# Relu² attention and mixture of depths on one core: chosen rows read back from DRAM instead of picked by matmul, in a new written-out order

## The chip, the cores and the metric

The kernel runs on one core of a Trainium2 chip. The metric is the time of one execution on the device in microseconds (us); lower is better. Five engines each run their own instructions in order: PE (TensorE, the matmuls), DVE (VectorE), ACT (ScalarE), POOL (GpSimd; here mostly the issue of DMAs) and SP (the issue of a few DMAs). They wait for one another by semaphores. PE writes its results into PSUM; DVE and ACT carry them from there to SBUF ("evict" them).

## The reference

Attention with squared relu over 8 batches, 12 heads, 448 tokens, 64 columns a head; its output, with the heads side by side as 768 columns, is x. Then, in each batch, the 128 tokens with the largest gate score go through a two-layer expert, and its result, weighted by a sigmoid, is added to their rows.

```python
scores = scale * q @ k.T                        # per head, scale = 1/sqrt(64)
x_heads = (np.maximum(scores, 0.0) ** 2 / S) @ v
x = heads side by side                          # [8, 448, 768]
s = x @ w_gate                                  # [8, 448]
for b in range(8):
    top_idx = the 128 tokens with the largest s[b]
    xe = x[b, top_idx]
    ye = np.maximum(xe @ w1, 0.0) @ w2          # 768 -> 1024 -> 768
    g = sigmoid(s[b, top_idx])
    out[b] = x[b];  out[b, top_idx] += g[:, None] * ye
```

## The kernel before

**Units.** The work is cut into 24 units: four heads of one batch each, unit u being the heads 4(u mod 3) to 4(u mod 3)+3 of batch u // 3. The 448 tokens of a unit are seven chunks of 64. One PSUM tile `ps` has eight banks, which the order hands out by number.

**The order** is written out by hand: ORDER is a list of tokens, and each token is a call that puts its instructions on one engine. Nothing reorders them; each engine has the tokens that concern it, in the order of the list. In the names below u is a unit, b a batch, c a chunk, and a last letter A or D says that ACT or DVE evicts. Evictions go through `put`, so in a profile of the kernel before their line is that of the helper: L209 for ACT, L211, L213 and L215 for DVE.

- `L,q,u`, `L,k,u`, `L,v,u` (L107) and `W` (L130): loads on POOL, cast to bf16 on the way. POOL's DMAs go round eight semaphores, and an issue waits for the DMA before it on the same one. q and k of unit 0 come by SP as float32 (`LFq`, L115; `LFk`, L118) and are cast by DVE (`Cq`, L195) and by DVE and ACT (`Ck`).
- `PW,n` (L202): n warm-up products of zeros on PE.
- `T,u,0` and `T,u,1` (L225): 14 transposes each, of q and of k, and `TE` their copy to `qkt`.
- `S,u,c` (L243): the scores of chunk c, four products of 448 columns; `R,u,c`: their relu eviction to `r_sb` (168 in all, ACT does them); `Q,u,c0,c1` (L257): the squares of chunks c0 to c1-1 on DVE, into `a_sb`, three instructions a unit; `V,u,c` (L264): four products with v, that sum over the chunks; `X,u` (L272): the eviction of the unit's output, columns down the partitions, to `xT_sb`.
- `RT,u` (L281): eight transposes of `xT_sb` to rows, `RE,u` (L289) their eviction to `x_rows`; `ST,b` (L305, L306): two DMAs that store the batch's rows in `out`.
- The gate and the choice: `g,b,i` (L326) six products with the gate weights, which stand repeated in `wg_rep`, so that each partition of PSUM gets the score row; `bc` its eviction to `bc_sb` (float32); `col` (L336) and `colE` (L341) the scores as columns, `rk` (L348), `cs0`, `cs` (L354, L360), `rank` (L365) the rank of every token, `hot` (L370) the one-hot matrix of the chosen tokens, `sel` (L376) and `sE` (L381) their indices `idx`.
- The expert: `xe,b,c` (L389): 24 products of `x_rows` with `hot`, which pick the chosen tokens' rows and transpose them; `xeE` their eviction to `xeT`; `gs` and `sig` (L404, L409) the weight; `h,b,f` (L416) six products with w1 each, `hE` their eviction; `y,b,f` (L432) products with w2, `yE` their eviction with the weight, to `gye`; `ADD,b` (L445): one indirect DMA on POOL that adds `gye` to the chosen rows of `out`.

The experts of a batch run among the attention of later units. Behind the last batch's `y` products only the last `yE` and `ADD,7` are left.

## Time and profile before

| | before |
|---|---|
| time, median of 3 runs (lowest to highest) | 206.81 us (206.43 to 207.01) |
| the profiled execution's own time | 206.75 us |
| span in its trace | 205.0 us |
| mean granted TensorE clock over the span | 0.989 |
| HBM read and written, over the span | 39.33 and 14.16 MB, 261 GB/s |

The trace covers the span; what lies between it and the profiled execution's own time, 1.75 us, is outside the trace. "Busy" is time in which an engine runs an instruction; PE's weight loads (PEld) run beside its products. A row "a 0.90 PE ps L225 x28" in the chain says that at a us the chain ran through 28 products of line 225 on PE for 0.90 us. A timeline's row can stand for several neighbouring instructions of one kind (x20), and its bracket says how long the engine was idle before it and what released it.

### The profile page before, as it was taken

How to read it: one execution, taken by the hardware profiler on the slowest of the kernel's cores; microseconds unless marked ns; L12 is line 12 of the kernel's file. 1: busy time of each engine (PE TensorE's matmuls, PEld its weight loads, DVE VectorE, ACT ScalarE, POOL GpSimd, SP SyncE). 2: the span in 40 equal slices, each digit the busy share in tenths (PEclk: the TensorE clock that was granted, in tenths of full speed). 3: DMA queues.
4: the chain of work that ended last, by engine and by line, in shares of the span. 5: the costliest groups of instructions: out<-in, count | busy, mean ns of one | idle time of the engine just before them, and what ended most of it. 6: DMA issues, size and time to landing. Idle time of an engine off the chain costs nothing.

```text
span 205.0 us, 7282 instructions
## 1 busy us (share of the span) xinstructions
PE 190.1 (93%) x3205; PEld 131.0 (64%) x3205; DVE 172.9 (84%) x285; ACT 170.8 (83%) x215; POOL 82.2 (40%) x120
## 2 busy tenths in 40 slices
...
GB/s 179 155 199 193 204 206 205 210 202 207 204 178 48 136 201 161 4 89 322 343 204 159 95 104 308 302 337 210 193 13 233 39 52 41 68 261 266 170 23 53
...
## 3 DMA queue, kind: packets, MB, share of 16 engines
...
q14 instruction: 6, 0.05, 0.1%
HBM read 39.33 MB, written 14.16 MB: 261 GB/s over the span
## 4 chain that ended last, share of the span: by engine, by line
PE 82%; DVE 8%; ACT 4%; issue 1%; POOLq 1%; DVEq 0%
PE ps L243 17%; PE ps L264 13%; PE ps L416 11%; PE ps L432 11%; PE ps L225 9%; PE ps L389 6%; PE ps L281 5%; DVE a_sb L257 4%; ACT r_sb L209 4%; PE ps L326 4%; PE ps L202 3%; DVE qkt L213 2%; PE ps L336 1%; POOLq L590 1%; DVE mask_sb L348 1%
## 5 line engine op out<-in xcount | busy, mean ns | idle before, releaser
L209 ACT ACTIVATE r_sb<-ps 128x896 bf16<-128x896 f32 x168 | 141.8, 942 | 8.7 <-PE ps L243 7.5
L257 DVE TENSOR_TENSOR a_sb<-r_sb 128x1792 bf16<-128x1792 bf16 (+1 forms) x72 | 87.1, 1238 | 0.0
L243 PE MATMUL ps<-qkt 64*64 64x448 bf16 x672 | 54.0, 360 | 2.6 <-ACT r_sb L209 0.9
L264 PE MATMUL ps<-a_sb,v_sb 64*64 64x448 bf16 x672 | 42.4, 351 | 0.4 <-ACT r_sb L209 0.2
L243 PEld LDWEIGHTS <-qkt 64*64 64x64 bf16 x672 | 20.8, 104 | 20.7 <-issue 10.3
L213 DVE COPY qkt<-ps 128x1792 bf16<-128x1792 bf16 (+1 forms) x24 | 25.5, 1068 | 2.7 <-PE ps L225 2.3
L264 PEld LDWEIGHTS <-v_sb 64*64 64x64 bf16 x672 | 20.7, 106 | 9.8 <-issue 1.5
L107 POOL DMA_DIRECT2D v_sb<-in_v_dram x24 | 17.4, 724 | 23.3 <-PE ps L243 18.6
L445 POOL DMA_INDIRECT out_dram<-gye,idx x8 | 13.4, 1675 | 32.6 <-DVE cols L341 8.8
L416 PE MATMUL ps<-xeT,w_sb 128*128 128x128 bf16 x384 | 25.0, 219 | 0.4 <-ACT xeT L209 0.4
L416 PEld LDWEIGHTS <-w_sb 128*128 128x128 bf16 x384 | 21.9, 98 | 4.9 <-issue 3.8
L107 POOL DMA_DIRECT2D q_sb<-in_q_dram x23 | 17.5, 761 | 18.2 <-PE ps L225 14.3
L432 PE MATMUL ps<-w_sb,hT 128*128 128x384 bf16 x128 | 24.7, 326 | 0.0
L107 POOL DMA_DIRECT2D k_sb<-in_k_dram x23 | 16.7, 729 | 9.7 <-PE ps L225 5.9
L215 DVE TENSOR_SCALAR xT_sb<-ps 128x896 bf16<-128x896 f32 x13 | 14.1, 1088 | 1.9 <-PE ps L264 1.6
L432 PEld LDWEIGHTS <-hT 128*128 128x128 bf16 x128 | 10.6, 97 | 7.3 <-issue 2.1
L225 PE MATMUL ps<-ident,q_sb 128*64 128x128 bf16 x336 | 14.1, 224 | 0.8 <-ACT r_sb L209 0.7
L225 PEld LDWEIGHTS <-q_sb 128*64 128x64 bf16 x336 | 10.7, 111 | 6.4 <-issue 4.9
L305 POOL DMA_DIRECT2D out_dram<-x_rows x8 | 5.0, 625 | 24.0 <-ACT r_sb L209 17.5
L281 PE MATMUL ps<-ident,xT_sb 128*128 128x128 bf16 x192 | 14.3, 220 | 0.0
L281 PEld LDWEIGHTS <-xT_sb 128*128 128x128 bf16 x192 | 11.2, 98 | 4.1 <-issue 3.0
L225 PE MATMUL ps<-ident,k_sb 128*64 128x128 bf16 x336 | 13.6, 219 | 0.0
...
## 6 DMA issues: line engine op xcount, KB each, us to landing
...
```

What stands on the lines that cost most here:

```text
L107: nc.gpsimd.dma_start(out=dst, in_=src(t, u))
L209: nc.scalar.activation(out=out_, in_=in_, func=func or AF.Copy, scale=scale)
L213: nc.vector.tensor_copy(out=out_, in_=in_)
L215: nc.vector.tensor_scalar(out=out_, in0=in_, scalar1=scale, scalar2=None, op0=ALU.mult)
L225: nc.tensor.matmul(out=PSB[HALF[j], bank, n * 128:(n + 1) * 128], lhsT=s[:, j, c, :], rhs=ident, is_transpose=True, start=(n == 0), stop=( ...
L243: nc.tensor.matmul(out=PS[HALF[hf], bank + j, :S], lhsT=qkt[u][HALF[j], 1, c, hf, :], rhs=qkt[u][HALF[j], 0, :, hf, :], start=True, stop=True)
L257: nc.vector.tensor_tensor(out=a_sb[u][:, c0:c1], in0=r, in1=r, op=ALU.mult)
L264: nc.tensor.matmul(out=PS[HALF[j], at["V", u] + hf, :S], lhsT=v_sb[u % NBUF][HALF[hf], j, c, :], rhs=a_sb[u][HALF[hf], c, j, :], start=(c ...
L281: nc.tensor.matmul(out=rows[:, c, g], lhsT=xT_sb[b % NX][:, 2 * uu + g, c, :], rhs=ident, is_transpose=True, start=(g == 0 and c == 0), st ...
L416: nc.tensor.matmul(out=PS[:, self.at["h"] + bk, o:o + 128], lhsT=w1_sb[:, m, f * 128:(f + 1) * 128], rhs=self.xeT[:, m, :], start=(m == 0) ...
L432: nc.tensor.matmul(out=PS[:, self.at["y"] + w, :384], lhsT=self.hT[:, f, :], rhs=w2_sb[:, f, w * 384:(w + 1) * 384], start=(f == 0), stop= ...
L445: nc.gpsimd.indirect_dma_start(out=out[0:self.b + 1].rearrange("b s d -> (b s) d"), out_offset=bass.IndirectOffsetOnAxis(ap=self.idx[:, :1 ...
```

## The change

1. **Chosen rows are read back.** For the batches 0 to 6 (READ), `XG,b` is an indirect DMA on POOL that reads the 128 chosen rows from `out`, where `ST,b` has stored them, into `xg` (bf16), and `XT,b` transposes `xg` by six products into PSUM. They take the place of the 24 products of `xe`. The read waits for `ST,b` and for `idx`; the transposes wait for the read. For batch 7 `xe` stays.
2. **Batch 7's scores** (DIRECT) come as columns straight from `xT_sb` (`colx`, 24 products of one column), and `rk` reads the score row in PSUM, so `bc` falls away there.
3. **The gate weights** are no longer repeated in SBUF: `g` reads one column of `wg_col` with stride 0 as its 128 columns. `wg_rep` and its two copies on DVE are gone.
4. **Opening.** SP loads k of unit 0 in two parts, chunks 0 to 1 and 2 to 6. q is cast by halves on DVE and ACT, and k's casts, transposes (`TK`) and copies (`TKE`) follow the two parts; q's copy is in two pieces, on ACT and DVE (`TQE`). There are 71 warm-up products in place of 75, 32 of them at the start in place of 40. The memsets of `xT_sb`, `bc_sb` and `mask_sb` go from DVE to POOL.
5. **Squares** in two instructions a unit, chunks 0 to 2 and 3 to 6.
6. **Last scatter** `ADD,7` as two DMAs, one for each half of the 768 columns; `between` puts a memset of one number (`gap`) on POOL ahead of an indirect DMA that follows another. Scatters and reads are declared independent of those of other batches.
7. **A new ORDER** for everything.

```diff
+    READ = (0, 1, 2, 3, 4, 5, 6)
+    DIRECT = (7,)
...
-    wg_rep = [const.tile([128, NM, 128], BF16, name=f"wg_rep{i}") for i in range(2)]
-    wg_col = const.tile([128, NM], BF16)
+    wg_col = const.tile([128, 2, NM], BF16)
...
-    def LFk():
-        nc.sync.dma_start(out=kf.rearrange("p j c d -> p j (c d)"), in_=src(k, 0))
+    def LFk(c0, c1):
+        nc.sync.dma_start(out=kf.rearrange("p j c d -> p j (c d)")[:, :, c0 * Dh:c1 * Dh],
+                          in_=src(k, 0)[:, :, c0 * Dh:c1 * Dh])
...
+    def between():
+
+        if last[0] in ("XG", "ADD"):
+            nc.gpsimd.memset(gap, 0.0)
...
-            nc.tensor.matmul(out=PS[:, self.at["g"], :S], lhsT=wg_rep[self.b not in BYDMA][:, i, :],
-                             rhs=self.xT[:, i].rearrange("p c n -> p (c n)")[:, :S], start=(i == 0), stop=(i == NM - 1),
-                             skip_group_check=True)
+            nc.tensor.matmul(out=PS[:, self.at["g"], :S],
+                             lhsT=wg_col[:, 1, i:i + 1].to_broadcast([128, 128]), rhs=self.xT[:, i].rearrange("p c n -> p (c n)")[:, :S],
+                             start=(i == 0), stop=(i == NM - 1), skip_group_check=True)
...
+        def colx(self, u, bank=None):
+            if u == 0:
+                self.at["col"] = bank
+            for m in (2 * u, 2 * u + 1):
+                for c in range(NR):
+                    nc.tensor.matmul(out=PS[:, self.at["col"], c:c + 1], lhsT=self.xT[:, m, c, :],
+                                     rhs=wg_col[:, 1 - (self.b in BYDMA), m:m + 1],
+                                     start=(m == 0 and c == 0),
+                                     stop=(m == NM - 1), skip_group_check=True)
...
+        def XG(self):
+            between()
+            self.xg = moe_pool.tile([CAP, HD], BF16, name="xg")
+            read = reads[self.b] = nc.gpsimd.indirect_dma_start(
+                out=self.xg, out_offset=None,
+                in_=out[0:self.b + 1].rearrange("b s d -> (b s) d"),
+                in_offset=bass.IndirectOffsetOnAxis(ap=self.idx[:, :1], axis=0),
+                element_offset=self.b * S * HD)
+            for b, add in adds:
+                tc.declare_no_dep(read.ins, add.ins, reason="rows of another batch")
+
+        def XT(self, bank):
+            self.at["xe"] = bank
+            for m in range(NM):
+                nc.tensor.matmul(out=PSB[:, bank, 128 * m:128 * m + 128],
+                                 lhsT=self.xg[:, 128 * m:128 * m + 128], rhs=ident,
+                                 is_transpose=True, start=(m == 0), stop=(m == NM - 1),
+                                 skip_group_check=True)
...
-        def ADD(self):
-            nc.gpsimd.indirect_dma_start(
-                out=out[0:self.b + 1].rearrange("b s d -> (b s) d"),
+        def ADD(self, part=None):
+            between()
+
+
+            w = 1 if part is None else 2
+            n = HD // w
+            add = nc.gpsimd.indirect_dma_start(
+                out=out[0:self.b + 1].rearrange("b s (w d) -> (b s w) d", w=w),
                 out_offset=bass.IndirectOffsetOnAxis(ap=self.idx[:, :1], axis=0),
-                in_=self.gye, in_offset=None, element_offset=self.b * S * HD,
-                compute_op=ALU.add)
+                in_=self.gye[:, (part or 0) * n:(part or 0) * n + n], in_offset=None,
+                element_offset=self.b * S * HD + (part or 0) * n, compute_op=ALU.add)
...
-    Zz PW,40,0 Zi Zs LFq LFk Ck,1 Cq T,0,0,0 Zt Ck,0 Zx PW,7,2 T,0,1 TE,0,1,D TE,0,0,A PW,13,2 S,0,0,0 R,0,0,A
+    LFq Zz LFk,0,2 Cq,0 Zi Zs Zt Ck,0,2,D PW,32,0 LFk,2,7 Cq,1 T,0,0,0 TQE,0,4,A TQE,4,7,D Zm TK,0,2 L,k,1 L,q,1
```

The new order shows best as each engine's own instructions. DVE at the very start, before (the names are the tiles written, and what they are read from):

```order
L136 MEMSET zero 128x64
L137 MEMSET unit_f 1x1
L195 CAST q_sb_83<-qf 128x896
L213 CAST k_sb_89<-kf 128x448
L146 MEMSET xT_sb_101 128x6x32
...
L148 MEMSET bc_sb_104 128x64
...
L213 COPY qkt<-ps 128x896
L176 CAST ident_119<-ident 6x6
L187 CAST wg_col<-ps 128x6
L188 CAST wg_rep_110<-ps 128x768
```

And the same stretch of DVE in the changed kernel:

```order
L141 MEMSET zero 128x64
L142 MEMSET unit_f 1x1
L217 CAST q_sb_85<-qf 128x448
L217 CAST k_sb_91<-kf 128x2x128
L217 COPY qkt<-ps 128x384
L217 COPY qkt<-ps 128x256
L217 CAST k_sb_91<-kf 128x2x320
L217 COPY qkt<-ps 128x640
L184 CAST ident_f<-ident 6x6
L271 TENSOR_TENSOR a_sb<-r_sb 128x2688
```

The cast of q is half as wide, k's cast and copy are in two pieces (two chunks and five), and the memsets and the gate weights' copies are gone from between.

POOL around the fifth read (batch 4), in the changed kernel, with the semaphores that each instruction waits for (DMASW0 to 7 are the eight of POOL's DMAs):

```order
L526 DMA out_dram<-gye,idx 896x768 [waits DMASW5_49,Activation_49]
L111 DMA v_sb_99<-in_v_dram 128x2x448 [waits DMASW6_49,PE_49]
L319 DMA out_dram<-x_rows 64x3072 [waits DMASW7_49,DVE_49]
L320 DMA out_dram<-x_rows 64x2304 [waits DMASW0_49]
L450 DMA xg<-out_dram,idx 128x768 [waits DMASW1_49,DMASW7_49,DMASW0_49,DVE_49]
L111 DMA v_sb_98<-in_v_dram 128x2x448 [waits DMASW2_49]
L111 DMA v_sb_101<-in_v_dram 128x2x448 [waits DMASW3_49,PE_49]
L111 DMA v_sb_100<-in_v_dram 128x2x448 [waits DMASW4_49]
```

The read (L450) waits for both stores of its batch (DMASW7, DMASW0) and for DVE's index, and three loads of v stand behind it, the first that of unit 19 (`v_sb_98`). In the kernel before these loads of v stand among other loads, ahead of the scatter of batch 2:

```order
L107 DMA v_sb_96<-in_v_dram 128x2x448 [waits DMASW1_49]
L107 DMA v_sb_98<-in_v_dram 128x2x448 [waits DMASW2_49,PE_49]
L107 DMA q_sb_86<-in_q_dram 128x2x448 [waits DMASW3_49]
L107 DMA v_sb_97<-in_v_dram 128x2x448 [waits DMASW4_49]
L107 DMA k_sb_93<-in_k_dram 128x2x448 [waits DMASW5_49]
L107 DMA v_sb_99<-in_v_dram 128x2x448 [waits DMASW6_49,PE_49]
L445 DMA out_dram<-gye,idx 1344x768 [waits DMASW7_49,Activation_49]
```

There no load has an index to wait for.

POOL at the end, before:

```order
L445 DMA out_dram<-gye,idx 2240x768 [waits DMASW4_49,DMASW3_49,Activation_49]
L445 DMA out_dram<-gye,idx 2688x768 [waits DMASW2_49,DMASW4_49,DMASW1_49,DMASW5_49,DVE_49,Activation_49]
L305 DMA out_dram<-x_rows 64x3072 [waits DMASW6_49]
L306 DMA out_dram<-x_rows 64x2304
L305 DMA out_dram<-x_rows 64x3072 [waits DMASW0_49,DVE_49,Activation_49]
L306 DMA out_dram<-x_rows 64x2304
L445 DMA out_dram<-gye,idx 3136x768 [waits DMASW6_49,DMASW7_49,DMASW5_49,DVE_49]
L445 DMA out_dram<-gye,idx 3584x768 [waits DMASW1_49,DMASW0_49,DMASW2_49,DVE_49,Activation_49]
```

And in the changed kernel:

```order
L319 DMA out_dram<-x_rows 64x3072 [waits DVE_49,Activation_49]
L320 DMA out_dram<-x_rows 64x2304
L526 DMA out_dram<-gye,idx 2240x768 [waits DMASW7_49]
L327 MEMSET gap 1x1 [waits Pool_49]
L526 DMA out_dram<-gye,idx 2688x768 [waits DMASW0_49]
L327 MEMSET gap 1x1 [waits Pool_49]
L526 DMA out_dram<-gye,idx 3136x768 [waits DMASW4_49,Activation_49]
L327 MEMSET gap 1x1 [waits Pool_49]
L526 DMA out_dram<-gye,idx 7168x384 [waits DMASW5_49,DMASW6_49,DVE_49,Activation_49]
L327 MEMSET gap 1x1 [waits Pool_49]
L526 DMA out_dram<-gye,idx 7168x384 [waits DMASW3_49,Activation_49]
```

The stores of the last batch now stand ahead of the scatters of the batches 4 to 6, the last batch's scatter is two DMAs of 384 columns, and the first of them waits for the index (DVE) and the first half of `gye` (ACT), the second only for the second half.

## Rows read from the trace of the kernel before

**Rows 1.** The page's first part: busy time, share of the span, instructions.

```profile
span 205.0 us, 7282 instructions
PE 190.1 (93%) x3205; PEld 131.0 (64%) x3205; DVE 172.9 (84%) x285; ACT 170.8 (83%) x215; POOL 82.2 (40%) x120
```

**Rows 2.** Windows: stretch, its length, busy time of each engine, clock, DMA.

```profile
core 0: us, PE busy (x) PEld busy (x) DVE busy (x) ACT busy (x) POOL busy (x), PEclk, DMA share, GB/s
8.50:20.00 11.50, 9.91 (x193) 6.43 (x185) 10.31 (x20) 11.50 (x15) 7.71 (x11) 1.00 1.23 192
20.00:40.00 20.00, 18.02 (x322) 10.71 (x319) 19.86 (x25) 20.00 (x26) 10.05 (x16) 1.00 1.22 205
40.00:140.00 100.00, 99.81 (x1729) 68.44 (x1729) 95.84 (x150) 93.66 (x117) 43.47 (x63) 1.00 0.95 191
```

**Rows 3.** Timeline of the end: start, length, engine, line, operation, [idle before].

```profile
189.41 0.16 DVE L381 TENSOR_REDUCE idx<-ps 128x1 int32<-128x2 f32 x1 [1.08 <-PE ps L376]
...
189.85 1.62 POOL L445 DMA_INDIRECT out_dram<-gye,idx  x1 [2.50 <-DVE idx L381]
...
194.74 0.65 PE L432 MATMUL ps<-w_sb,hT 128*128 128x384 bf16 x3
...
196.87 1.56 POOL L445 DMA_INDIRECT out_dram<-gye,idx  x1 [5.39 <-DVE gye L215]
```

**Rows 4.** Timeline: the first score group of unit 9.

```profile
61.87 0.36 PE L243 MATMUL ps<-qkt 64*64 64x448 bf16 x4
```

**Rows 5.** Timeline of the opening.

```profile
0.95 0.06 DVE L137 MEMSET unit_f<- 1x1 f32 x1
1.06 4.45 PE L202 MATMUL ps<-zero 128*128 128x128 bf16 x40 [1.06 <-DVE unit_f L137]
3.94 0.63 DVE L195 CAST q_sb<-qf 128x896 bf16<-128x896 f32 x1 [2.94 <-DMA qf<-in_q_dram]
5.44 0.75 PE L225 MATMUL ps<-ident,q_sb 128*64 128x128 bf16 x14
6.07 0.39 DVE L213 CAST k_sb<-kf 128x448 bf16<-128x448 f32 x1 [1.50 <-DMA kf<-in_k_dram]
8.04 0.76 PE L243 MATMUL ps<-qkt 64*64 64x448 bf16 x12
8.47 17.11 ACT L209 ACTIVATE r_sb<-ps 128x896 bf16<-128x896 f32 x21 [1.02 <-PE ps L243]
```

**Rows 6.** The chain that ended last: start, length, engine, what, line, instructions.

```profile
45.75 0.90 PE ps L225 x28
46.65 0.50 PE ps L243 x8
48.51 1.11 PE ps L416 x18
55.89 0.69 PE ps L243 x12
57.47 1.41 PE ps L432 x8
84.79 1.00 PE ps L281 x16
90.48 1.45 PE ps L389 x24
```

**Rows 7.** Groups of instructions by line and shape: busy, mean ns, idle before.

```profile
L209 ACT ACTIVATE r_sb<-ps 128x896 bf16<-128x896 f32 x168 | 141.8, 942 | 8.7 <-PE ps L243 7.5 <-DVE a_sb L257 0.4
L257 DVE TENSOR_TENSOR a_sb<-r_sb 128x1792 bf16<-128x1792 bf16 x48 | 51.2, 1082 | 0.0
L257 DVE TENSOR_TENSOR a_sb<-r_sb 128x2688 bf16<-128x2688 bf16 x24 | 37.2, 1549 | 0.0
L404 PE MATMUL ps<-wg_col,xeT 128*128 128x1 bf16 x48 | 2.3, 163 | 0.0
```

**Rows 8.** The loads' line L107: issue in ns (least/median/most), then landing.

```profile
L107 POOL DMA_DIRECT2D q_sb<-in_q_dram x23: 696/722/1385, 3.1 to 133.2; - x23
...
DMA to landing us min/median/max: 3.6/7.7/10.9
```

**Rows 9.** The scatters' line L445, the same columns.

```profile
L445 POOL DMA_INDIRECT out_dram<-gye,idx x8: 1543/1652/1893, 105.2 to 196.9; - x8
...
DMA to landing us min/median/max: 5.5/5.7/6.0
```

**Rows 10.** Windows of 0.5 us behind the last scatter's issue.

```profile
199.00:199.50 0.50, 0.00 (x0) 0.00 (x0) 0.00 (x0) 0.00 (x0) 0.00 (x0) 1.00 1.45 135
...
201.00:201.50 0.50, 0.00 (x0) 0.00 (x0) 0.00 (x0) 0.00 (x0) 0.00 (x0) 0.50 0.85 160
201.50:202.00 0.50, 0.00 (x0) 0.00 (x0) 0.00 (x0) 0.00 (x0) 0.00 (x0) 0.50 0.12 18
```

292 lines of the change are left out of this document (166 added, 126 removed).

## The prediction

> **What bounds the kernel now.** I read the page's busy times first, then the stages, then single instructions. The page says that PE is busy 93% of the span, DVE 84% and ACT 83% [rows 1]; none of the three can be dropped from the argument. The stages tell them apart [rows 2]. Between 8.5 and 20 us ACT is busy for the whole 11.50 us, and between 20 and 40 us ACT and DVE have 20.00 and 19.86 of 20 us, while PE has 18.02: the front, which has only attention to do, is paced by the two engines that empty PSUM. From 40 to 140 us PE has 99.81 of 100 us, with DVE at 95.84 and ACT at 93.66: there PE sets the pace, with the others close behind. PE's last matmul ends at 194.74 + 0.65 = 195.39 [rows 3], and behind it stands only the last scatter.
>
> So a microsecond of PE work is worth a microsecond only after the front; in the front the first eviction's time and ACT's work count. I cut at S,9,0, the first score group of unit 9, at 61.87 us [rows 4]: about there PE takes over, and both orders have the same evictions before it.
>
> **The opening.** Today PE runs 40 warm-up products until 5.5 us, q is cast at 3.94 and k, whole, at 6.07; the first scores start at 8.04 and the first eviction at 8.47, from where ACT runs without a gap [rows 5]. In the new order 32 warm-ups end near 1.06 + 32 x 0.111 = 4.6. The first two of seven key chunks should land at 3.94 + 2/7 x (6.07 - 3.94) = 4.55. q's transposes (0.75 us in the old opening's place, half of the 28 in 0.90 at speed [rows 6]) then end near 5.3, their copies by 5.9, the four k transposes and their copy by 6.2; nine warm-ups stand ahead of the first scores, which I put at 6.7, and the first eviction at 7.15: 1.3 earlier. Up to S,9,0 ACT has the same 62 evictions in both, and one gate-row copy more in the new order (about 0.3, an estimate by the 942 ns of an eviction twice its width, less what was idle [rows 7]). I take **-1.0**; ends: 0 if the split keys land no earlier, -1.3 if the extra copy hides.
>
> **PE's work.** Removed: 24 selection products in each of seven batches, 1.45 us a batch [rows 6], 10.2 in all. Added: 42 transposes at the same 0.06, 2.5. Batch 7's scores come straight from columns: 24 one-column products for 4, by the gate's products (48 in 2.3 us [rows 7]) at most 1.2 more, I take 0.6. Four warm-ups fewer save 0.4, in the front. That is 7.5 less in sum, but not all of it lies where PE is the bound. The new order starts the experts later: before S,9,0 the old one has already done batch 0's selection, its 48 products of w1 (18 in 1.11: 3.0), its 16 of w2 (8 in 1.41: 2.8) and 6 for its gate (0.3); the new one has only ten V groups (four products of 448 columns, as a score group; 0.19 each, what 12 in 0.69 have over 8 in 0.50) and one pair of transposes (0.45) more [rows 6]. Behind S,9,0 therefore: -8.7 (six batches' selection), +2.5, +0.6, +5.7 (batch 0's 6.1 moved in, less the 0.1 that each of these rows has at its start), -2.35: **-2.3**. Ends: 0 if DVE and ACT take over, -5 if the front is not paced by ACT after all, so that what was saved there counts too.
>
> **What must follow PE.** Squares go from three instructions a unit to two. 1792 columns take 1082 ns, 2688 take 1549 [rows 7], so 0.467 per 896 and 0.148 fixed; 24 instructions fewer save DVE 3.55 us. DVE also loses the gate-row copies, the replicated gate weights and the memsets, and takes three row copies from ACT for two xT evictions that go to ACT. I give this no term: it is the cover for the -2.3, since DVE's idle 4.2 us in 40 to 140 would otherwise not suffice for a faster PE. The memsets go to POOL, four of them ahead of the third load; by a load's issue (722 ns [rows 8]) at most 2.9 us, hidden because unit 1's transposes come only near 10 us; without that cover the opening's 1.0 is lost. The gate weights read with stride 0: nothing, or one 0.06 slot for each of 48 products, 2.9; I take nothing, for the same number of columns is loaded.
>
> **The seven reads.** A read can be issued when the batch's rows are stored and its index is reduced, and PE's transposes, in order, wait for it: everything behind them on PE (scores, so ACT's evictions, so DVE's squares) waits too. On POOL the loads behind it wait until the index comes. No indirect read is in the trace. The nearest rows are the eight indirect scatters: 1.54 to 1.89 us to issue, 5.5 to 6.0 us from start to landing [rows 9]. From the reduction (0.16) to the scatter's start took 189.85 - 189.57 = 0.28 [rows 3], so data should stand 6.1 us after the reduction starts. The new order leaves PE for batch 4, between reduction and transposes: 7 S, 4 V, 28 + 16 transposes, 14 products of w2: 1.33 + 0.76 + 0.90 + 1.0 + 2.3 = 6.3 [rows 6], and some 0.1 at each change of kind, 6.9. The other batches have 6.6 to 7.5, batch 3 some 11. So each just fits. Behind the fifth read stands the load of v of unit 19, whose first use follows that read's transposes: from 2.0 after the reduction, when the read is issued, to some 8, 6 us, against landings of 3.6 to 10.9, median 7.7 [rows 8]; the queues are emptier there than in most of those. **+0.5** for the seven reads and this load. Ends: 0, and 8 (below).
>
> **The last scatter.** Today: last matmul 195.39, scatter's start 196.87, issue 1.56 [rows 3], data from 199.0 to about 201.6 [rows 10], span's end 205.0: 9.6 behind PE. With halves the first can start some 0.2 after PE's end, as its eviction runs beside the second half's products; its issue, 1.6, pushes the second's start to 2.0 and its end to 3.6, 0.55 later than today. The data behind it are half of 2.6, 1.3 less: **-0.7**. The one-number memset put between the two I count at nothing (0.06 on DVE [rows 5]). Ends -1.3 and +0.6. The Trainium skill, page "DMA: Bandwidth & Descriptors", section "Anatomy of one DMA", fits such a transfer as about 2.0 us and bytes by 436 per ns; by it half of 393 KB saves an estimated 0.45, and the sum of this part would be +0.1 in place of -0.7. The trace's long data phase speaks for the larger saving.
>
> **The sum** is made against the profiled execution, 206.75 us (span 205.0 and 1.75 around it), 0.06 under the median of the runs, 206.81: 206.75 - 1.0 - 2.3 + 0.5 - 0.7 = 203.25, **203.3** against the median.
>
> **Rivals.**
> *The reads come late* (the other side). Seven in-order waits at the places above. The plain loads show the price: 7.7 us median from start to landing, 10.9 at most, with up to eight DMAs queued [rows 8]. If a read queues like that and takes 8, six of the seven batches wait 1.0 to 1.9, 8 in all: 211. Near 7.0 the waits sum to 3.5 or so and eat the gain; that is the point from which it decides. For it: in the first 60 us the new POOL order has the reads behind full queues. Against: all eight scatters landed within 6.0 [rows 9].
> *Slow issue.* One load's issue took 1385 ns where 722 is the median [rows 8], so POOL is at times held up. Were every read's issue doubled, by 1.65, the waits would be about 5: 208. The Trainium skill, page "SBUF — State Buffer", section "SBUF: two separate sides", gives a cause: GpSimd cannot write descriptors while VectorE holds the port that they share; by that rule the sum would be this rival's. Against it stand eight indirect issues of at most 1.89 beside a DVE that is busy 96%.
> *The evicting engines take over at once.* PE's -2.3 becomes idle time: 205.6. For it: ACT at 94% and DVE at 96% already; against: DVE's 3.55.
> *The opening or the halves do nothing*: 204.3 or 204.0.
>
> **Chances.** The forecast with its terms' own spread (201 to 205): 0.55. Engines take over: 0.17. Opening or halves empty: 0.08. Reads late or issued slowly: 0.20, of which 0.13 end above 207.4, 0.05 within 0.3% and 0.02 below. A measurement tells from no change about 0.3%, 0.6 us. The evicting case lies in part within that bound (0.03). So faster 0.79, same 0.08, slower 0.13. The range that leaves out 2 in 10 goes from 200.6 (the forecast with the front's saving counting half) to 206.9 (reads that eat the gain); the forecast's own is 201 to 205.
>
> **What would show it.** First eviction near 7.15 and S,9,0 near 60.9. PE without idle time from there, and its last matmul near 192.4. Before each group of xg transposes PE idle under 0.3; waits of 1 us or more there mean the first rival, and the indirect issues' durations part it from the second. If PE shows gaps in front of scores released by ACT or DVE, the third. Span's end 8.9 behind PE's last matmul, with the first half's data moving before the second is issued. The forecast is wrong if any read lands more than 7 us after it starts, or if S,9,0 does not move.

## The result, and the profile after

The changed kernel takes 204.31 us at the median of 20 executions (202.58 to 207.81), the kernel before 206.62 in as many on the same chips (206.32 to 208.01). The ratio is 0.9857, 95% interval 0.9834 to 0.988: 1.4% faster; times 206.62 that is 203.7, against the forecast of 203.3 and its range of 200.6 to 206.9. The ratio leaves out executions over 1.5% above the kernel's fastest; the profiles of experiments 2, 4, 6 and 7 fell on such ones, so single stages are compared there, not spans. The profiled execution took 202.62 us and is one of the fastest: what it shows is 4.1 us, while the typical execution gained 2.3 by the medians and 3.0 by the ratio.

The page's first part, after:

```profile
span 200.9 us, 7058 instructions
PE 183.7 (91%) x3095; PEld 124.7 (62%) x3095; DVE 166.1 (83%) x256; ACT 168.4 (84%) x216; POOL 96.8 (48%) x141
```

The last of the windows of [rows 2], behind the front:

```profile
40.00:140.00 100.00, 97.48 (x1726) 65.42 (x1721) 94.81 (x139) 96.83 (x125) 48.25 (x64) 1.00 1.06 208
```

From 40 to 140 us PE was busy 99.81 of 100 us and now is 97.48; ACT went from 93.66 to 96.83. PE has lost most of its lead.

The opening, to hold against [rows 5], the first score group of unit 9, against [rows 4], and the end, against [rows 3], all from the timeline:

```profile
1.07 3.59 PE L206 MATMUL ps<-zero 128*128 128x128 bf16 x32 [1.07 <-DVE unit_f L142]
4.07 0.58 ACT L213 ACTIVATE q_sb<-qf 128x448 bf16<-128x448 f32 x1 [1.76 <-DMA qf<-in_q_dram]
4.61 0.27 DVE L217 CAST k_sb<-kf 128x256 bf16<-128x256 f32 x1
4.75 0.75 PE L230 MATMUL ps<-ident,q_sb 128*64 128x128 bf16 x14
6.78 0.57 PE L257 MATMUL ps<-qkt 64*64 64x448 bf16 x8 [0.57 <-DVE qkt L217]
7.22 4.97 ACT L213 ACTIVATE r_sb<-ps 128x896 bf16<-128x896 f32 x6 [1.08 <-PE ps L257]
...
59.93 0.39 PE L257 MATMUL ps<-qkt 64*64 64x448 bf16 x4
...
190.39 1.46 PE L508 MATMUL ps<-w_sb,hT 128*128 128x384 bf16 x8
191.48 1.56 POOL L526 DMA_INDIRECT out_dram<-gye,idx  x1 [1.89 <-ACT gye L213]
192.46 0.62 POOL L327 MEMSET gap<- 1x1 f32 x1
193.34 1.56 POOL L526 DMA_INDIRECT out_dram<-gye,idx  x1 [0.26 <-issue]
```

These rows cut the span at the places of the prediction:

| us | before | after | difference | forecast |
|---|---|---|---|---|
| to S,9,0 | 61.87 | 59.93 | -1.94 | -1.0 |
| S,9,0 to the end of PE's last matmul | 133.52 | 131.92 | -1.60 | -2.3 + 0.5 |
| from there to the span's end | 9.65 | 9.02 | -0.63 | -0.7 |

They add up to -4.17, the difference of the spans, which are 205.04 and 200.87 to the hundredth (the expectations below still have 9.05, from spans to the tenth). The windows from S,9,0 to PE's last matmul and from there to the end, before and then after (columns as in [rows 2]), part the second line into work and waiting:

```profile
61.87:195.39 133.52, 133.01 (x2259) 92.95 (x2254) 118.38 (x199) 114.74 (x145) 46.44 (x59) 1.00 0.77 167
195.39:205.04 9.65, 0.00 (x0) 0.00 (x0) 0.62 (x1) 0.34 (x1) 1.56 (x1) 0.76 0.28 41
```

```profile
59.93:191.85 131.92, 130.96 (x2178) 90.46 (x2167) 114.50 (x186) 112.74 (x146) 56.20 (x71) 1.00 0.86 176
191.85:200.87 9.02, 0.00 (x1) 0.00 (x0) 0.00 (x0) 0.58 (x1) 2.79 (x3) 0.75 0.46 64
```

PE's busy time fell by 2.05 us, where the sum had -2.3; its idle time rose from 0.51 to 0.96.

The reads by their line (issue in ns, then landing), and the one place where a read was waited for, from the timeline:

```profile
L450 POOL DMA_INDIRECT xg<-out_dram,idx x7: 992/1032/2551, 53.9 to 170.0; - x7
DMA to landing us min/median/max: 3.8/4.5/7.8
```

```profile
99.83 0.34 PEld L461 LDWEIGHTS <-xg 128*128 128x128 bf16 x6 [0.32 <-DMA xg<-out_dram,idx]
99.83 0.51 PE L461 MATMUL ps<-ident,xg 128*128 128x128 bf16 x6
```

Five of seven reads took 1.0 us to issue; the two long issues are taken up below. PE itself waited for none of the reads: the only wait is 0.32 us of the weight loads (PEld), which run beside PE's products. From start to landing the seven took 4.5, 3.9, 5.8, 7.8, 5.9, 3.8 and 3.9 us, and their transposes started 1.8, 2.1, 0.04, 0.7, 0.9, 1.9 and 2.6 us after the landing. The fourth read, with 7.8, meets the sign that the prediction had set for being wrong, a read that lands more than 7 us after it starts. It cost nothing, because 11.4 us lie there between index and transposes, where the other six have 6.1 to 7.0.

### The profile page after: what moved, and what is told of

Its sections match the earlier page's. It is cut to its first block, busy times and chain, and to the rows that moved or that the text cites. A ratio compares the mean times of both kernels' runs of the same rounds, so it can differ in the third digit from the quotient of the medians.

```text
span 200.9 us, 7058 instructions
## 1 busy us (share of the span) xinstructions
PE 183.7 (91%) x3095; PEld 124.7 (62%) x3095; DVE 166.1 (83%) x256; ACT 168.4 (84%) x216; POOL 96.8 (48%) x141
## 4 chain that ended last, share of the span: by engine, by line
PE 44%; DMA 17%; DVE 13%; ACT 9%; POOL 7%; issue 5%; POOLq 1%; DVEq 0%; ACTq 0%
DMA q_sb<-in_q_dram 12%; PE ps L492 8%; PE ps L257 8%; PE ps L508 8%; ACT r_sb L213 8%; PE ps L278 7%; DVE a_sb L271 6%; DMA k_sb<-in_k_dram 5%; PE ps L230 4%; PE ps L295 4%; DVE qkt L217 3%; PE ps L347 2%; POOL k_sb L111 1%; POOL xg L450 1%; DVE xT_sb L219 1%
## 5 line engine op out<-in xcount | busy, mean ns | idle before, releaser
L271 DVE TENSOR_TENSOR a_sb<-r_sb 128x2688 bf16<-128x2688 bf16 (+1 forms) x48 | 84.9, 1786 | 2.7 <-ACT r_sb L213 1.9
L257 PE MATMUL ps<-qkt 64*64 64x448 bf16 x672 | 55.1, 360 | 4.5 <-DVE qkt L217 1.9
L257 PEld LDWEIGHTS <-qkt 64*64 64x64 bf16 x672 | 21.4, 104 | 23.0 <-issue 11.5
L450 POOL DMA_INDIRECT xg<-out_dram,idx x7 | 10.0, 1429 | 43.3 <-DVE idx L434 43.0
L217 DVE COPY qkt<-ps 128x1792 bf16<-128x1792 bf16 (+3 forms) x26 | 26.0, 1006 | 3.6 <-PE ps L230 1.8
L278 PEld LDWEIGHTS <-v_sb 64*64 64x64 bf16 x672 | 21.6, 106 | 10.0 <-issue 2.8
L508 PE MATMUL ps<-w_sb,hT 128*128 128x384 bf16 x128 | 24.4, 326 | 0.0
L111 POOL DMA_DIRECT2D q_sb<-in_q_dram x23 | 18.3, 812 | 10.7 <-PE ps L230 10.4
L111 POOL DMA_DIRECT2D k_sb<-in_k_dram x23 | 17.9, 779 | 10.8 <-PE ps L230 7.5
L111 POOL DMA_DIRECT2D v_sb<-in_v_dram x24 | 19.0, 799 | 4.1 <-DMA k_sb<-in_k_dram 1.2
L526 POOL DMA_INDIRECT out_dram<-gye,idx x9 | 15.4, 1713 | 6.3 <-ACT gye L213 3.9
L230 PE MATMUL ps<-ident,q_sb 128*64 128x128 bf16 x336 | 14.1, 223 | 1.3 <-DMA q_sb<-in_q_dram 0.8
L295 PE MATMUL ps<-ident,xT_sb 128*128 128x128 bf16 x192 | 14.1, 219 | 0.0
L230 PE MATMUL ps<-ident,k_sb 128*64 128x128 bf16 x336 | 13.9, 219 | 0.3 <-DMA k_sb<-in_k_dram 0.3
L217 DVE COPY x_rows<-ps 128x1024 bf16<-128x1024 bf16 x20 | 13.4, 684 | 0.4 <-ACT r_sb L213 0.4
```

What stands on the lines that cost most here:

```text
L111: nc.gpsimd.dma_start(out=dst, in_=src(t, u))
L217: nc.vector.tensor_copy(out=out_, in_=in_)
L230: nc.tensor.matmul(out=PSB[HALF[j], at["T", u, w], n * 128:(n + 1) * 128], lhsT=s[:, j, c, :], rhs=ident, is_transpose=True, start=(n == 0 ...
L257: nc.tensor.matmul(out=PS[HALF[hf], bank + j, :S], lhsT=qkt[u][HALF[j], 1, c, hf, :], rhs=qkt[u][HALF[j], 0, :, hf, :], start=True, stop=True)
L271: nc.vector.tensor_tensor(out=a_sb[u][:, c0:c1], in0=r, in1=r, op=ALU.mult)
L278: nc.tensor.matmul(out=PS[HALF[j], at["V", u] + hf, :S], lhsT=v_sb[u % NBUF][HALF[hf], j, c, :], rhs=a_sb[u][HALF[hf], c, j, :], start=(c ...
```

## The experiments

The theory: in the kernel before PE sets the pace behind S,9,0, so its work there is worth its time, DVE and ACT being close behind; the reads fit. The rivals: the evicting engines (DVE, ACT) set the pace now, or the reads and the loads behind them do. No experiment has the reads alone or the opening alone in the kernel before, so what each is worth by itself is read from the places of the span and not shown by a run. The best ruler turned out to be the seven groups of `xg` transposes. This table has the times between the starts of neighbouring groups, from the timeline of PE in each profile (the first column is the start of the first group, the last runs to the end of PE's last matmul):

| us | to 1st | 1-2 | 2-3 | 3-4 | 4-5 | 5-6 | 6-7 | to PE's end |
|---|---|---|---|---|---|---|---|---|
| changed kernel | 60.25 | 20.7 | 18.8 | 23.6 | 25.5 | 13.9 | 13.6 | 15.3 |
| 1, the same again | 60.25 | 20.7 | 18.8 | 24.1 | 25.5 | 13.9 | 13.6 | 15.3 |
| 2, last scatter as one DMA | 61.85 | 22.0 | 18.8 | 24.4 | 25.5 | 13.9 | 13.6 | 15.3 |
| 3, keys in one part | 61.20 | 20.7 | 18.8 | 24.4 | 25.5 | 13.9 | 13.6 | 15.3 |
| 4, three squares | 63.79 | 20.9 | 19.1 | 24.0 | 25.7 | 14.0 | 13.6 | 15.3 |
| 5, 18 more products a read | 60.44 | 21.7 | 19.8 | 24.4 | 26.4 | 14.9 | 14.5 | 16.3 |
| 8, 16 fewer products of w1 | 60.36 | 20.7 | 18.8 | 25.1 | 25.5 | 13.9 | 12.8 | 14.3 |
| 6, reads later, two memsets | 62.05 | 20.9 | 20.2 | 28.9 | 25.8 | 14.1 | 13.5 | 15.3 |
| 7, reads later, six memsets | 65.75 | 24.7 | 24.2 | 26.1 | 28.2 | 17.7 | 17.5 | 16.8 |
| 9, opening's loads | 60.42 | 21.4 | 18.8 | 24.1 | 25.5 | 14.0 | 13.5 | 15.7 |
| 10, q of unit 16 first | 61.73 | 21.1 | 20.0 | 23.5 | 25.4 | 14.1 | 13.6 | 15.7 |
| 11, both | 60.78 | 20.9 | 20.4 | 23.4 | 25.5 | 14.2 | 13.5 | 15.7 |

### Is PE the bound? Experiments 5, 8 and 4

**5.** The transposes of each read four times over:

```diff
-            for m in range(NM):
+            for m in list(range(NM)) * 4:
                 nc.tensor.matmul(out=PSB[:, bank, 128 * m:128 * m + 128],
                                  lhsT=self.xg[:, 128 * m:128 * m + 128], rhs=ident,
```

> The changed kernel with each group of six xg transposes done four times over into the same place: 126 more products of 128 columns on PE, about 7.2 us at the 0.057 of a row like 24 in 1.36, as many as the picking products that the change removed. Theory (PE is the bound behind the front): 5.5 to 7.5 us slower, about 4 us slower than the kernel before. Rival (the evicting engines are the bound, PE has slack): under 3 us slower, at about the time of the kernel before or faster.

Measured: 210.03 us, ratio to the kernel before 1.0174 (1.0148 to 1.0199); against the 0.987 of experiment 1 that is 3.0% or 6.3 us more, 7.0 us of work having been added (18 products take 1.0 us: 24 in 1.50 us there, 6 in 0.51). Each stage after the first group is 0.7 to 1.0 us longer than in the first profile of the changed kernel. The theory's range (5.5 to 7.5) holds, the rival falls. So the picking products that the change removed would cost nearly their full time in the new order.

**8.** Four of the six products of each group of w1; the last 256 columns of the chosen rows are left out:

```diff
-            for m in range(NM):
+            for m in range(4):
...
-                                 start=(m == 0), stop=(m == NM - 1), skip_group_check=True)
+                                 start=(m == 0), stop=(m == 3), skip_group_check=True)
```

> The changed kernel with four of the six products of each w1 group (the last 256 columns of the chosen rows are left out of the first layer): 128 fewer products of 128 columns, 7.4 us less on PE, spread over all batches. Theory (PE is the bound, others close behind): 2 to 4 us faster, with PE waiting for ACT and DVE in 40 to 140 us. Rival 1 (PE has been the only bound): 6 to 7.4 us faster. Rival 2 (the evicting engines already set the pace): under 1.5 us faster, of which 1.0 is the last batch's own path behind attention.

Measured: 203.97 us, ratio 0.9793 (0.9749 to 0.9836): 0.8% below experiment 1's 0.987, 1.6 us of 7.4, with overlapping intervals. The table says where: only the last two stages got shorter, by 0.8 and 1.0, and stage 3-4 got longer. The windows between the groups, of the changed kernel (columns as in [rows 2]):

```profile
60.25:80.99 20.74, 20.58 (x354) 13.77 (x350) 19.70 (x32) 20.74 (x28) 10.16 (x17) 1.00 1.12 215
...
99.83:123.47 23.64, 23.27 (x390) 15.17 (x390) 20.36 (x24) 21.64 (x29) 15.41 (x18) 1.00 1.14 210
123.47:148.99 25.52, 25.20 (x458) 17.28 (x456) 25.49 (x42) 25.00 (x33) 7.76 (x10) 1.00 0.64 137
...
162.89:176.51 13.62, 13.61 (x202) 9.43 (x199) 11.06 (x19) 8.39 (x13) 1.03 (x2) 1.00 0.56 149
```

And of experiment 8:

```profile
60.36:81.10 20.74, 20.06 (x338) 13.12 (x334) 19.71 (x32) 20.74 (x28) 10.21 (x17) 1.00 1.12 217
99.85:124.92 25.07, 22.74 (x376) 14.42 (x374) 20.34 (x24) 21.53 (x29) 17.62 (x18) 1.00 1.16 213
124.92:150.43 25.51, 24.93 (x442) 16.57 (x440) 25.44 (x42) 24.99 (x33) 7.75 (x10) 1.00 0.56 123
```

Read the fourth and fifth numbers (DVE, ACT): in 1-2 ACT is busy 20.74 of 20.74 us in both kernels, in 4-5 DVE 25.49 of 25.52 and 25.44 of 25.51. There PE's lighter work became idle time. In 5-6, which kept its 13.9 us, neither is full (12.48 and 13.20 of 13.89 us in experiment 8), and what held that stage is not shown. In 6-7 DVE and ACT have 11.06 and 8.39 of 13.62 and PE 13.61: there PE alone sets the pace, and a product less is time less. In 3-4 PE waited 1.9 us for q of unit 16 in experiment 8 and 0.33 in the changed kernel: all came earlier but the load. The first rival of this experiment (6 to 7.4) falls; in the total, 1.6 us, the theory (2 to 4) and the second rival (under 1.5) can't be told apart. By the stages the second fits up to the sixth read, the theory behind it. Experiment 5 says that PE is as close: after the change the three engines are close to balance, more on PE costs at once and less gains little.

**4.** The squares in three pieces, as many instructions as before the change:

```diff
-        r = r_sb[u][:, c0:c1]
-        nc.vector.tensor_tensor(out=a_sb[u][:, c0:c1], in0=r, in1=r, op=ALU.mult)
+        for d0, d1 in ((0, 3),) if c0 == 0 else ((3, 5), (5, 7)):
+            r = r_sb[u][:, d0:d1]
+            nc.vector.tensor_tensor(out=a_sb[u][:, d0:d1], in0=r, in1=r, op=ALU.mult)
```

> The changed kernel with the squares in three instructions a unit (chunks 0 to 2, 3 to 4, 5 to 6): 24 more DVE instructions, 3.55 us of DVE. Theory (PE sets the pace behind the front, DVE's fewer instructions are only its cover): 0 to 1 us slower. Rival (DVE is the bound in the middle): 2.5 to 3.5 us slower.

Measured: 205.08 us, ratio 0.9882 (0.9838 to 0.9927), no difference to 0.987 that the intervals allow. From the first group to PE's last matmul it takes 132.7 us, against 131.6 and 132.0 in the two profiles of the changed kernel. The theory (0 to 1 us) holds and the rival (2.5 to 3.5) falls: DVE's 3.55 us were mostly cover. The 63.79 of its front is another matter, below.

### How much room do the reads have? Experiments 6 and 7

POOL copies the index and sets memory ahead of each read, so that the read starts later:

```diff
+            self.idy = tiny.tile([CAP, 1], INT32, name="idy")
+            nc.gpsimd.tensor_copy(out=self.idy, in_=self.idx)
+            for _ in range(2):
+                nc.gpsimd.memset(fill, 0.0)
...
-                in_offset=bass.IndirectOffsetOnAxis(ap=self.idx[:, :1], axis=0),
+                in_offset=bass.IndirectOffsetOnAxis(ap=self.idy[:, :1], axis=0),
```

with six in place of two in experiment 7. In experiment 6 the two memsets took 1.10 us and the copy 0.18, but 1.91 beside a square, so that four of the reads start 1.2 to 1.4 us later after their index than in the changed kernel, the third and the fifth 2.8 and 3.0, and the fourth, which had waited its turn on POOL, no later.

> The changed kernel with a POOL copy of the index and two memsets of 128x512 ahead of each read, about 1.2 us more between index and read. Landings of 4.5 us at the median leave 1.5 to 2 us of slack by the prediction's sums of 6.6 to 7.5: theory, 0 to 1 us slower, PE's waits for xg under 1.5 us in all. Rival (the reads just fit, as forecast): 0.8 us at six of the seven, 4 to 6 us slower.

> The same with six memsets, about 3.2 us more between index and read. Theory (slack of 1.5 to 2 us): waits of 1 to 2 us at six of seven reads, 7 to 11 us slower if each wait is a loss, of which the evictions behind make up little. Rival (what waits on PE is made up by the engines that were behind it): under 5 us slower.

Measured: 210.75 us with two memsets, ratio 1.0112 (1.0077 to 1.0147), 5 us above the changed kernel by the ratios and 6.4 by the medians; 232.08 with six, 28 us above. The times of the theory fall both times. With two memsets PE waited 1.5 us for reads, nearly all at the third (1.28 us); the theory had under 1.5, the rival waits at six of seven. That the total lies in the rival's range (4 to 6) is luck, for the largest loss came from a load: q of unit 16 stands behind the third read on POOL, came late with it, and PE waited 2.96 us for it. Stage 3-4 got 5.3 us longer than in the first profile of the changed kernel, and only half of that is waiting:

```profile
103.12:132.01 28.89, 25.89 (x390) 16.19 (x390) 19.59 (x23) 20.43 (x27) 19.49 (x22) 0.88 1.13 201
```

PE did the same 390 products there in 25.89 us that took 23.27 in the changed kernel, at a granted clock (the third number from the right) of 0.88 in the mean. With six memsets PE waited for six reads, 15.8 us in all, up to 4.59 at once. What such a wait does is in the timeline and the windows of experiment 7 around the third read; the last row has everything from S,9,0 to PE's last matmul:

```profile
114.65 0.82 PE L466 MATMUL ps<-ident,xg 128*128 128x128 bf16 x6 [4.59 <-DMA xg<-out_dram,idy]
```

```profile
112.00:114.00 2.00, 0.00 (x0) 0.00 (x0) 0.00 (x0) 0.00 (x0) 2.00 (x4) 0.66 0.84 101
117.00:119.00 2.00, 2.00 (x15) 0.64 (x12) 2.00 (x4) 1.51 (x2) 0.07 (x1) 0.50 1.14 418
63.00:220.93 157.93, 138.41 (x2176) 92.50 (x2167) 115.11 (x186) 114.27 (x146) 86.85 (x120) 0.95 0.77 151
```

The granted clock falls from 1.00 to 0.50, 2.4 to 1.2 GHz, while PE stands still, and is still 0.50 when PE has been busy again for over 4 us: the six transposes take 0.82 us in place of 0.51. Not every wait is paid again in this way. Behind the waits for the third and the last three reads the clock was at 0.50 for 3.5 to 7 us; behind those for the first two (2.37 and 1.72 us) it stayed at 1.00. From S,9,0 to PE's last matmul the time is 26.0 us longer than in the changed kernel: 18.6 of it is PE's idle time, for reads and for loads, and 7.4 slower work; another 3.1 us lie ahead of S,9,0. In both profiles of the changed kernel, where PE waits at most 0.80 us for a load and for no read, the clock stays at 1.00 until PE's last matmul.

### What holds a read up

The seven issues fall into two kinds. The third read of the changed kernel beside the first, with what DVE did, from the timeline:

```profile
53.66 1.09 DVE L217 COPY qkt<-ps 128x1792 bf16<-128x1792 bf16 x1
53.92 1.04 POOL L450 DMA_INDIRECT xg<-out_dram,idx  x1 [4.07 <-DVE idx L434]
...
93.41 2.02 DVE L271 TENSOR_TENSOR a_sb<-r_sb 128x3584 bf16<-128x3584 bf16 x1
93.95 2.35 POOL L450 DMA_INDIRECT xg<-out_dram,idx  x1 [0.83 <-DVE idx L434]
```

Beside a copy out of PSUM the issue takes 1.04 us. Beside a square (SBUF to SBUF) it ends 96.30 - 95.43 = 0.87 behind the square's end. The fifth read is the other long one (142.24 + 2.55 against 141.88 + 2.01: 0.90 behind). Experiments 4 and 10, made for other ends, vary it: where the squares are cut in two (the third and the fifth read of experiment 4), and where the read begins late in the square (the third of experiment 10).

```profile
97.14 2.08 DVE L272 TENSOR_TENSOR a_sb<-r_sb 128x1792 bf16<-128x1792 bf16 x2
97.50 1.60 POOL L451 DMA_INDIRECT xg<-out_dram,idx  x1 [0.65 <-DVE idx L435]
...
146.36 2.08 DVE L272 TENSOR_TENSOR a_sb<-r_sb 128x1792 bf16<-128x1792 bf16 x2
146.72 2.62 POOL L451 DMA_INDIRECT xg<-out_dram,idx  x1 [16.14 <-DVE idx L435]
```

```profile
95.28 2.02 DVE L271 TENSOR_TENSOR a_sb<-r_sb 128x3584 bf16<-128x3584 bf16 x1
95.75 0.72 POOL L111 DMA_DIRECT2D q_sb<-in_q_dram  x1 [0.76 <-issue]
96.77 1.41 POOL L450 DMA_INDIRECT xg<-out_dram,idx  x1 [0.30 <-issue]
102.84 0.51 PE L461 MATMUL ps<-ident,xg 128*128 128x128 bf16 x6 [1.06 <-DMA xg<-out_dram,idx]
```

In experiment 4 the third read's issue ends at 99.10, 0.88 behind the first of the two squares (97.14 + 1.08); the fifth's at 149.34, 0.90 behind the second, having waited for both. In experiment 10 it ends at 98.18, 0.88 behind the square. In all profiles together 30 reads began while a square ran, and 29 ended 0.87 to 0.93 behind that square. So the issue waits until the square that runs when it begins is over, once for the next square too, and then takes its 0.9. The scatters do the same: 34 began beside a square and ended 1.4 to 1.65 us behind it. Plain loads do not wait. Two loads of the changed kernel, and the copy of the index in experiment 6, each with the square beside it:

```profile
98.55 2.02 DVE L271 TENSOR_TENSOR a_sb<-r_sb 128x3584 bf16<-128x3584 bf16 x1
98.83 1.49 POOL L111 DMA_DIRECT2D q_sb<-in_q_dram  x2
```

```profile
95.34 2.02 DVE L272 TENSOR_TENSOR a_sb<-r_sb 128x3584 bf16<-128x3584 bf16 x1
95.50 1.91 POOL L452 COPY idy<-idx 128x1 int32<-128x1 int32 x1 [0.44 <-DVE idx L435]
```

Both loads are issued within the square, in 0.75 us each; 29 of the changed kernel's 70 loads of q, k and v began beside a square, at the same median of 0.75 us as the others. The copy, 0.18 us elsewhere, ends 0.05 behind the square. What waits takes the index from SBUF, the copy and the reads alike; the loads, which don't wait, take none. The Trainium skill, page "SBUF — State Buffer", section "SBUF: two separate sides", says that VectorE and GpSimd share a port pair as an exclusive lock, and that an operation of VectorE with two SBUF inputs, as the square is, takes it only against an operation of GpSimd that reads SBUF; the trace agrees, with 0.87 to 0.93 us behind the square in 29 of 30 reads and loads that go on beside it. An order that puts no square behind those two indices wasn't tried.

### The opening and the loads. Experiments 1, 3, 9, 10 and 11

**1.** The changed kernel again.

> The changed kernel once more, for a second profile. Its executions ran from 202.6 to about 205 us, wider than those of the kernel before. If the spread comes from reads that land late in some executions, this profile, if its time is over 203.5, has PE waiting 0.5 us or more ahead of some xg transposes, beyond the 0.3 us of the first profile. If it comes from the loads of q and k in the first 60 us, the transposes of q and k wait longer than the 1.1 us of the first profile, S,9,0 starts later than 59.93, and the reads wait no more. If neither, PE's work from S,9,0 to its last matmul takes 131.9 us again and the difference is elsewhere.

Measured: 204.48 us (202.8 to 207.09), ratio 0.987 (0.9818 to 0.9921); the profile, of 203.0 us, fell on a short execution, so none of the three cases is decided by it. It repeats the first in every stage but 3-4, where T,16 waited 0.80 us for its q in place of 0.33.

**3.** Unit 0's keys in one load:

```diff
-    LFq Zz LFk,0,2 Cq,0 Zi Zs Zt Ck,0,2,D PW,32,0 LFk,2,7 Cq,1 T,0,0,0 TQE,0,4,A TQE,4,7,D Zm TK,0,2 L,k,1 L,q,1
+    LFq Zz LFk,0,7 Cq,0 Zi Zs Zt Ck,0,2,D PW,32,0 Cq,1 T,0,0,0 TQE,0,4,A TQE,4,7,D Zm TK,0,2 L,k,1 L,q,1
```

> The changed kernel with the first keys loaded in one part again; all else of the opening stays. Theory (first eviction sets the front): first eviction at about 8.5 in place of 7.22, S,9,0 later by 1.0 to 1.3, time 1.0 to 1.3 us longer. Rival (the front is paced by loads, which come no earlier): S,9,0 moves by less than 0.4 and the time by less than 0.4.

Measured: 204.84 us, ratio 0.989 (0.9842 to 0.9938). From its timeline:

```profile
5.90 0.29 DVE L217 CAST k_sb<-kf 128x256 bf16<-128x256 f32 x1 [1.20 <-DMA kf<-in_k_dram]
7.53 3.35 ACT L213 ACTIVATE r_sb<-ps 128x896 bf16<-128x896 f32 x4 [1.27 <-PE ps L257]
```

The first keys came 1.29 later than in the changed kernel (4.61), the first eviction only 0.31 later, and 0.94 earlier than before the change. Even the 0.31 is hardly outside what varies: with the split the first eviction lies between 7.00 and 7.43 in the other profiles. So by these rows the split load is the smaller part of the opening's gain at the first eviction; the larger is the shorter way from keys to scores: a cast, transposes and a copy of two chunks in place of seven, q cast on two engines and transposed from 4.75 in place of 5.44. No run takes the shorter way alone. S,9,0 came at 60.88, 0.95 later, and the time is 0.4 us longer by the ratios, within their intervals: neither the theory (first eviction at 8.5) nor the rival (S,9,0 moves by under 0.4) fits. PE waits in this front for loads, for q twice (0.16 and 0.32) and for k of unit 9 at 53.9 us (0.78), 1.26 us in all against 0.73 in the changed kernel; the rest of the 0.95 is open. The profile of the kernel before has no wait for a load in its front, that of experiment 12, in the old order, one of 0.58.

One such wait differs most from profile to profile, that of unit 3's transposes for q. Experiment 2's timeline, and its window there:

```profile
14.64 0.96 PE L230 MATMUL ps<-ident,q_sb 128*64 128x128 bf16 x14 [1.33 <-DMA q_sb<-in_q_dram]
```

```profile
14.00:15.00 1.00, 0.36 (x8) 0.36 (x10) 0.93 (x1) 1.00 (x2) 0.51 (x1) 0.52 1.26 201
```

PE waited 1.33 us for q of unit 3, the granted clock fell from 1.00 to 0.50, and the 14 transposes took 0.96 us in place of 0.58; its first read's transposes come at 61.85. At this place the profiles of experiments 2, 4, 6 and 7 have waits of 1.33, 2.12, 1.27 and 2.09 us, each with the clock at 0.50 for some microseconds around or behind it. Experiment 10 has 1.56 us, and the clock stayed at 1.00; the others have at most 0.94.

**9.** The memsets of xT behind the first loads, and q of unit 3 ahead of k of unit 2; **10.** q of unit 16 ahead of the third read; **11.** both:

```diff
-    Zh Lw Zx,1 T,1,1 Q,0,0,3 Zx,0 S,0,5,2
+    Zh Lw T,1,1 Q,0,0,3 S,0,5,2
...
-    R,1,1,A L,k,2 L,q,3 S,1,3,4
+    R,1,1,A L,q,3 L,k,2 S,1,3,4
...
-    R,1,4,A Q,1,0,3 L,k,4 Zg,4
+    R,1,4,A Q,1,0,3 L,k,4 Zx,1 Zx,0 Zg,4
```

```diff
-    L,q,17 hot,2,0 L,v,17 RT,10,3
+    L,q,17 hot,2,0 L,v,17 L,q,16 RT,10,3
...
-    L,q,18 L,q,16 sig,1
+    L,q,18 sig,1
```

> The changed kernel with two edits to POOL's opening: the two memsets of xT (0.81 us between the second and the third load) go behind the seventh load, and q of unit 3 is loaded ahead of k of unit 2. Theory (the transposes of unit 3 wait for q near 14 us, 0.3 to 2.1 us in the profiles so far, and that makes both the spread and part of the loss): no wait for q between 13 and 22 us, executions closer together, median 0.5 to 1.2 us below the changed kernel's. Rival (ACT and DVE set the pace in the front, the wait is covered): the wait goes, the time stays within 0.3 us.

> The changed kernel with q of unit 16 loaded ahead of the third read in place of behind it and behind two stores. Theory (the loads behind the read land late near 108 us: 0.3, 0.8, 1.0, 1.1, 0.7 and 1.9 us of wait so far, with DVE 16.7 and ACT 18.0 of 20 us busy between 100 and 120): the wait for q there goes, 0.4 to 1.0 us faster than the changed kernel. Rival (another thing of that stage, the work that PE has between, keeps ACT and DVE idle there): under 0.3 us.

> Both edits of the loads together. Theory: the two gains add up, 1.0 to 2.0 us below the changed kernel, executions within about 1 us of each other. Rival (what one gains the other loses, ACT and DVE being busy 20 of 20 us between): no more than the larger of the two alone.

Measured: 205.55, 205.74 and 205.27 us, ratios 0.994 (0.9909 to 0.997), 0.9922 (0.9882 to 0.9962) and 0.9906 (0.9878 to 0.9935). None is faster than the changed kernel, and the ratios are higher, though it did not run on the same chip as they. In 9 the wait for q of unit 3 is gone, but q of unit 2 is waited for next (0.45), then q of unit 11 (0.54), and the front stays at 60.4. Its executions lie 2.8 us apart (204.25 to 207.04), against 5.2 in the changed kernel and 4.3 in experiment 1, but it is the shortest that are missing; those of 11, with the same edit, lie 4.3 apart. So it is not shown that this wait makes the spread, and the theory's gain has fallen. In 10 and 11 the wait of T,16 is gone and stage 3-4 is down to 23.5 and 23.4, but stage 2-3 is 1.2 and 1.6 longer: PE waits 1.06 and 1.48 us for the third read. By the rows of experiment 10 above it starts 0.94 later after its index than in the changed kernel, behind the load, but the square holds its issue either way, and that ends 2.80 behind the index as there (2.82). What is later is the landing: the transposes start 4.7 us behind the issue's end, where the rows of the changed kernel landed 3.5 behind it. The load of q, issued right ahead of the read, is what the edit put there; that its data go before the read's is argued and not seen. What one gained the other lost.

### The last scatter. Experiments 2 and 12

**2.** One DMA again in the changed kernel (and the index without its factor of 2), **12.** halves alone in the kernel before (with the factor, and `gap`):

```diff
-    yE,7,1,A sE,7 ADD,7,0 ADD,7,1
+    yE,7,1,A sE,7 ADD,7
```

```diff
-    yE,7,0,D ADD,7
+    yE,7,0,D ADD,7,1 ADD,7,0
```

> The changed kernel with its last scatter as one DMA again. Theory (halves save data time, lose an issue): the span ends 9.6 us after PE's last matmul, as before, in place of 9.05; 0.5 to 0.7 us slower than the changed kernel. Rival (halves buy nothing, the gap memset and second issue eat it): within 0.2 us of the changed kernel.

> The kernel before with its last scatter alone as two halves of columns, each behind its own eviction, with the one-number memset between. Theory by the changed kernel's tail (the tail was 9.29 with one scatter and 9.05 with two there, since the second starts 1.86 after the first and the data phase is some 1.2 shorter): 0.0 to 0.3 us faster than before. Rival (the prediction's -0.7, the memset at nothing): 0.5 to 0.8 faster.

Measured: 204.77 us for 2, ratio 0.9877 (0.9838 to 0.9916), no difference to the changed kernel in the totals; 207.62 us for 12, ratio 1.0037 (1.0011 to 1.0062), slower. The tails behind PE's last matmul tell more: 9.02 and 9.03 in the two profiles of the changed kernel, 9.29 with one DMA there, 9.65 before, 10.08 with halves there. So by single profiles halves gain 0.27 in the new end and lose 0.43 in the old one. The gain is near what varies: with halves and the reads as they are the other profiles have 9.1 to 9.2, and experiment 8 has 9.7. In the old end the order finishes both halves of `y` together, and the first half's scatter starts only at 197.14, 1.1 behind PE's end:

```profile
197.14 1.58 POOL L452 DMA_INDIRECT out_dram<-gye,idx  x1 [4.99 <-DVE gye L218]
...
199.03 1.55 POOL L452 DMA_INDIRECT out_dram<-gye,idx  x1 [0.27 <-issue]
```

In the new one PE finishes the first half of `y` eight products earlier, and its scatter is under way when PE ends: it starts at 191.48, 0.37 ahead of PE's end, and the second 1.49 behind it, against 3.01 in experiment 12. For 2 the theory (0.5 to 0.7 slower) falls, and its rival (within 0.2) can't be excluded by the totals. For 12 the theory and the rival both fall: halves don't pay in the old end, and in the new one they gain some 0.3 us at best.

## Why the prediction was right, step by step

- **The opening**, -1.0 forecast. The first eviction came 1.25 earlier, as forecast (1.3), but S,9,0 1.94. The windows from the first eviction to S,9,0, before and after:

```profile
8.47:61.87 53.40, 49.68 (x858) 31.45 (x854) 51.31 (x75) 52.81 (x67) 26.89 (x41) 1.00 1.20 198
```

```profile
7.22:59.93 52.71, 47.26 (x861) 29.55 (x861) 49.66 (x64) 52.41 (x66) 31.68 (x50) 1.00 1.21 211
```

  ACT is busy for 52.81 of 53.40 us and then for 52.41 of 52.71, so it paces the front, as said; PE was idle there for 3.7 us and more. The size was wrong in ACT's work, which fell by 0.40 where I had it grow by 0.3: the second gate-row copy came (0.9 us more), but one eviction of xT fewer stands before the cut (1.0 less), which I had not counted. ACT's idle time fell by 0.29. The reason given for the first eviction was half right: the early landing of two chunks is worth some 0.3 there by experiment 3, and by its rows the short pieces are the rest.
- **PE's work**, -2.3: PE's busy time behind S,9,0 fell by 2.05. That this would be time holds for removing it from the kernel before (experiment 5 gives it back nearly whole). It would not have held for much more: the rival in which the evicting engines take over stood at the door, and in two of the stages, 1-2 and 4-5, ACT or DVE sets the pace by now.
- **The seven reads**, +0.5 for waits: PE had none for them, and its idle time rose by 0.45, of which 0.33 was a wait for q of unit 16. "Each just fits" was too strict for four reads, which had 1.8 to 2.6 us to spare, since I took the scatters' 5.5 to 6.0 and the reads landed in 4.5 at the median. For the third it was exact (0.04 us), and that it held there is luck: its issue was held up for 1.3 us, which the forecast hadn't allowed for. The landing in 7.8 us at the fourth, the first rival's case, fell on the one batch with 11 us of room. The place I named, v of unit 19 behind the fifth read, did not wait; q of unit 16, behind the third, did. The first rival's price was too low: reads that start 1.2 to 3 us later cost 5 us, and with four more memsets 28, since the loads behind them come late too and the clock falls.
- **Slow issue**, the second rival, is real in two reads of seven, 1.3 and 1.5 us each, and the room that the short landings left took it up. By the rows above it is not the writing of descriptors that waits, as I had it, since plain loads go on beside squares, but the reading of the index. The argument against it, eight scatters of at most 1.89 us beside a busy DVE, did not test it. Of those eight issues one began beside a square, and it is the second longest (median 1.65); the longest, 1.89, began beside another DVE operation on SBUF, `mask_sb`:

```profile
169.14 2.55 DVE L257 TENSOR_TENSOR a_sb<-r_sb 128x1792 bf16<-128x1792 bf16 x2
171.33 1.79 POOL L445 DMA_INDIRECT out_dram<-gye,idx  x1 [4.63 <-ACT x_rows L209]
```

- **The last scatter**, -0.7: -0.63, but the halves are 0.27 of it by experiment 2, and the other 0.36 is the new order of the end. I had 0.55 for the second scatter's later end and 1.3 saved in its data; against experiment 2 the last issue ends 0.61 later and the span's end follows it 0.88 sooner (5.96 us in place of 6.84). The memset that I counted at nothing shows 0.62 us on POOL, but 0.58 of that lies beside the issue before it: the second scatter starts 1.86 behind the first, 0.30 after its issue's end. By the fit of the Trainium skill's page "DMA: Bandwidth & Descriptors", section "Anatomy of one DMA", this part was to be an estimated +0.1; the measured saving of the halves lies between that and mine.
- **The covers**: the gate weights read with stride 0 cost nothing (353 ns for each of 48 products before and after). DVE's 3.55 us were mostly cover, as said. That POOL's memsets are hidden holds for unit 1 in the first profile; experiments 4 and 10 have waits of 0.22 and 0.68 us for its q, and experiment 9 gained nothing by moving two of the memsets.
- **The sum**: the terms came to -4.17 in the profiled execution, 0.7 more than forecast, and the typical execution gained 1 to 2 us less than that one, through a spread that the forecast did not have. That the two nearly cancel, so that 203.7 stands beside 203.3, is luck; the terms themselves held, with the sizes above.

Left open: why the changed kernel's executions spread over 5.2 us where those before spread over 1.7. The profiles of experiments 2 and 4 show waits for q with a lowered clock in the front, but in experiment 11, whose profile has no such wait in the front longer than 0.42 us, the executions still lie 4.3 us apart.
